# K's, V's and the late weights' loads issued by GpSimd, one packet per DMA engine, in a decode kernel with attention and a gated MLP

## The chip, the cores and the metric

The kernel runs on one core of one Trainium2 chip. The time is the device time in microseconds of one execution; the median of three runs of the kernel before is 2520.21 us (2520.2 to 2520.8). A profile of one execution shows what each engine did: TensorE (PE, with its weight loads PEld), VectorE (DVE), ScalarE (ACT), GpSimd (POOL), SyncE (SP), and the 16 DMA engines that move data between HBM and the on-chip memory.

## The reference

One token passes two branches, mixed by a gate. The attention branch reads a long cache: 32 heads, 65,536 cached tokens, 128 numbers each, in bfloat16, so K and V together are 1.07 GB that have to be read once.

```python
q = (x @ wq).reshape(B, Sq, H, Dh).transpose(0, 2, 1, 3)       # one token, H = 32, Dh = 128
scores = einsum("bhqd,bhkd->bhqk", q, k_cache) * Dh ** -0.5    # Sk = 65536
a = (softmax(scores) @ v_cache -> reshape) @ wo                # D = 512
b = (silu(x @ w_gate) * (x @ w_up)) @ w_down                   # F = 1792
g = sigmoid((x * gate_w).sum(-1))
out = g * a + (1 - g) * b
```

## The kernel before

The tokens of a head are split into two halves, z = 0 and z = 1, of 32,768 tokens. A half of K or of V is one load of 8 MiB: 128 partitions, each with a contiguous row of 256 tokens (64 KiB). All loads go into one large buffer `mem`, in blocks of 512 numbers per partition; `place` (L193 to L196) gives the block of each load. K's first half goes to block 32 (KA), K's second to 0 (KZ), V's first half to 120 (VA) and V's second to 96 (VZ). VA and VZ overlap by 40 blocks, KZ and KA by 32, so a load has to wait until the part that it overwrites has been used.

Work on a head runs as a software pipeline over the engines. VectorE transposes K in eight steps per half (L397 and L404; L329 for the first head), each into one of two buffers `kt`, and counts them in the semaphore `ktdone`. TensorE multiplies each transposed step with the query (L454, `scores`) and counts in `qkdone`. When both halves of a head have their scores, VectorE takes the maximum per partition (L343), GpSimd the maximum over the partitions (L273, `partition_all_reduce`), ScalarE the exponentials (L300) with their sums, and GpSimd the sum over the partitions (L275). VectorE rearranges the exponentials into `pb` with 16 small copies per half (L338, `shuffle`). TensorE then multiplies them with V of that head (L501), one head behind the scores, in two parts per half, and counts the parts in `pvdone`; `turn` (L481) and two ScalarE steps bring the head's result into a column.

The order of the loads is written out on SyncE (L209 to L245). The four weight loads `wq`, `wg`, `wu`, `wd` are issued ahead of everything (L203), then K's first half for head 0 in two loads of 4 MiB (L217), and then for each head, each behind a wait on `ktdone` or `pvdone`: K's first half, V's first half of the head before, K's second half, V's second half of the head before (all L213). The loads of the end are: 31 of the 32 rows of `wo` (L235), the last head's V in eight pieces from 4 MiB down to 128 KB (L242, table `tail`), and two loads of 128 KB from `wo` (L244, L245). All of these share one queue, SP's. ScalarE issues the token `x`, `gate_w` and the output.

GpSimd at the start builds small constants (L249 to L269, with `affine_select`), then does only the two reductions per head, in the order of heads (L272 to L275). VectorE and TensorE run their heads in a loop on their engine; what they wait for is given by counts of the semaphores.

Of the kernel before, what the change touches and what calls it, by code (L numbers as in the profile page):

```python
# [5 lines left out]
P = 128  # L6
KB = 512
PR = 32
NG = PR // 4

ALU = mybir.AluOpType
ACT = mybir.ActivationFunctionType
# [8 lines left out]
def bass_gated_mix__mha_block_cached__swiglu_ffn__decode_kernel(  # L21
# [11 lines left out]
    out: bass.AP,  # L33
):
    _, H, S, Dh = A_k_cache.shape
    D = A_wq.shape[0]
    F = B_w_gate.shape[1]
# [3 lines left out]
    HR = R // 2  # L41
    NP = HR // PR
# [5 lines left out]
    KA, KZ, VA, VZ, V0 = 32, 0, 120, 96, 96  # L48
# [10 lines left out]
    tail = [(32, 0, 128), (0, 128, 128), (V0 + 24, 256, 128), (V0 + 64, 384, 64),  # L59
            (V0 + 80, 448, 32), (V0 + 56, 480, 16), (V0 + 60, 496, 12), (V0 + 63, 508, 4)]  # L60
    WOJ, WO31 = V0, V0 + 1

    with ExitStack() as ctx:
# [6 lines left out]
        def sem(name):  # L70
            return ctx.enter_context(nc.semaphore(name))
# [35 lines left out]
        def at(kb, n):  # L107
            return mem[:, kb * KB:kb * KB + n]
# [9 lines left out]
        d = {n: sem("d_" + n) for n in names}  # L118
        dt_ = [sem(f"d_t{i}") for i in range(len(tail))]
# [16 lines left out]
        s_q = sem("s_q")  # L136
# [7 lines left out]
        s_b = sem("s_b")  # L144
        s_dch = sem("s_dch")
        ktdone = sem("ktdone")
        qkdone = sem("qkdone")
        pvdone = sem("pvdone")
# [26 lines left out]
        w_dram = {  # L175
            "wq": A_wq.rearrange("(p c) n -> p (c n)", c=Dc),
            "wg": B_w_gate.rearrange("(p c) f -> p (c f)", c=Dc),
            "wu": B_w_up.rearrange("(p c) f -> p (c f)", c=Dc),
            "wd": B_w_down.rearrange("(p c) n -> p (c n)", c=FC),
            "wo": A_wo.rearrange("(p j) n -> p (j n)", p=P),  # L180
        }
        wj_dram = w_dram["wo"][:, 31 * D:32 * D]
        w31_dram = A_wo.rearrange("(h d) n -> h d n", d=Dh)[H - 1]
        WQ, WG, WU, WD, WO = V0, 0, 14, V0 + 64, 64
# [5 lines left out]
        w2_ap = at(WOJ, 2 * D).rearrange("p (e c n) -> p e c n", e=2, c=4)  # L190
        ktb = [kt[:, b, :].bitcast(BF16).rearrange("p (j r m e) -> p j r m e", j=2, r=NG, e=2) for b in range(2)]

        def place(kind, h, z):  # L193
            if kind == "k":
                return (KA, V0)[z] if h == 0 else (KA, KZ)[z]
            return (VA, VZ)[z]  # L196

        def kv_dram(cache, h):
            return cache[0, h].rearrange("(b p r) d -> b p (r d)", b=2, p=P)

        for n, kb in (("wq", WQ), ("wg", WG), ("wu", WU), ("wd", WD)):
            src = w_dram[n]
# [3 lines left out]
        ctx.callback(lambda: nc.scalar.wait_ge(s_out, 16))  # L206
        block = ctx.enter_context(nc.Block())

        @block.sync  # L209
        def _(sp):  # L210
            def load(kind, h, z):
                cache = A_k_cache if kind == "k" else A_v_cache
                sp.dma_start(at(place(kind, h, z), HR * Dh), kv_dram(cache, h)[z]).then_inc(d[kind + "az"[z]], 16)  # L213

            half = HR // 2 * Dh
            for n in range(2):
                sp.dma_start(at(KA + 32 * n, half), kv_dram(A_k_cache, 0)[0][:, n * half:n * half + half]).then_inc(  # L217
                    (d["ka0"], d["ka"])[n], 16)
            sp.wait_ge(s_q, 1)
            load("k", 0, 1)  # L220
            for h in range(1, H):
                sp.wait_ge(ktdone, 2 * NP * h - 3 if h > 1 else NP)
                load("k", h, 0)
                if h == 1:
                    sp.wait_ge(ktdone, 2 * NP - 3)
                    sp.wait_ge(s_b, 1)
                else:
                    sp.wait_ge(pvdone, 4 * h - 1)
                load("v", h - 1, 0)
                sp.wait_ge(ktdone, 2 * NP * h + NP // 2)  # L230
                load("k", h, 1)
                sp.wait_ge(pvdone, 4 * h + 1)
                load("v", h - 1, 1)
            sp.wait_ge(ktdone, 2 * NP * H - NP)
            sp.dma_start(at(WO, 31 * D), w_dram["wo"][:, 0:31 * D]).then_inc(d["wo"], 16)  # L235
            src = A_v_cache[0, H - 1].rearrange("(b p r) d -> b p (r d)", b=2, p=P)
            need = {0: (ktdone, 2 * NP * H - 3), 1: (ktdone, 2 * NP * H), 2: (pvdone, 4 * H - 1)}
            for n, (kb, r0, nr) in enumerate(tail):
                if n in need:
                    sp.wait_ge(*need[n])  # L240
                b, o = divmod(r0, HR)
                sp.dma_start(at(kb, nr * Dh), src[b][:, o * Dh:(o + nr) * Dh]).then_inc(dt_[n], 16)  # L242
            sp.wait_ge(pvdone, 4 * H)
            sp.dma_start(at(WOJ, D), wj_dram).then_inc(d["wj"], 16)  # L244
            sp.dma_start(at(WO31, D), w31_dram).then_inc(d["w31"], 16)  # L245

        @block.gpsimd
        def _(pool):
            nc.gpsimd.memset(onesf[0:1, :], 1.0)  # L249
            nc.gpsimd.memset(sel, 0.0).then_inc(s_sel0, 1)  # L250
            pool.wait_ge(s_sel0, 1)
            for je in range(4):
                off = 64 * (je // 2) + je % 2
                v = sel[:, je, :].rearrange("p (g d) -> p g d", g=4)
                last = nc.gpsimd.affine_select(out=v, in_=v, compare_op=ALU.not_equal, fill=1.0, base=-off,
                                               pattern=[[0, 4], [-2, 32]], channel_multiplier=1)
            last.then_inc(s_sel, 1)
            nc.gpsimd.memset(unit[:], 0.0).then_inc(s_unit0, 1)
            pool.wait_ge(s_unit0, 1)
            nc.gpsimd.affine_select(out=unit[:], in_=unit[:], compare_op=ALU.not_equal, fill=1.0, base=0,  # L260
                                    pattern=[[-1, 4]], channel_multiplier=1).then_inc(s_unit, 1)
            nc.gpsimd.memset(bmat[:], 0.0).then_inc(s_b0, 1)
            for q in range(4):
                pool.wait_ge(s_b0, q + 1)
                nc.gpsimd.affine_select(out=bmat[:], in_=bmat[:], compare_op=ALU.not_equal, fill=1.0, base=-32 * q,
                                        pattern=[[-1, 32]], channel_multiplier=1).then_inc(s_b0, 1)
            nc.gpsimd.memset(hot[0:1, :, :], 0.0).then_inc(s_hot0, 1)
            pool.wait_ge(s_hot0, 1)
            nc.gpsimd.affine_select(out=hot[0:1, :, :], in_=hot[0:1, :, :], compare_op=ALU.not_equal, fill=1.0,  # L269
                                    base=0, pattern=[[1, 4], [-1, 4]], channel_multiplier=0).then_inc(s_hot, 1)  # L270
            for h in range(H):
                pool.wait_ge(s_mx, h + 1)  # L272
                nc.gpsimd.partition_all_reduce(amx, mxs, P, RMAX).then_inc(s_ar, 1)  # L273
                pool.wait_ge(expdone, h + 1)
                nc.gpsimd.partition_all_reduce(Lt, rsum, P, RADD).then_inc(s_L, 1)  # L275

        @block.scalar
        def _(act):
# [148 lines left out]
        def _(pe):  # L427
# [22 lines left out]
            def scores(z, c, u):  # L450
                col = 256 * z + PR * u
                for r in range(NG):
                    for je in range(4):
# [129 lines left out]
```

## Time and profile before

| | |
|---|---|
| median of three runs | 2520.21 us |
| span of the profiled execution, first to last instruction | 2518.7 us |
| the profiled execution's own time | not given apart from its span; the median lies 1.5 us above the span |
| moved by the DMA engines | 1088.00 MB, mean 432 GB/s |
| share of the 16 engines' span, SP's queue | 99.9% |
| PE, DVE, ACT, POOL busy | 63%, 55%, 3%, 1% |
| PE weight loads busy | 35% |
| mean granted TensorE clock | 0.711 |
| loads of 8 MiB, K and V | 63 and 62 |

A line of the timeline gives the start in us from the span's beginning, the duration, the engine and line, the operation, what it writes and reads, and in brackets how long the engine stood idle before it and what ended that wait. SPq is SP's issuing of a DMA. A line of the DMA issues ends with the time in us from the issue to the landing of the data. In the chain of waits a line is a start, a length and what the chain went through in that time. A group of instructions gives busy time, mean duration in ns, and the idle time ahead of it with its releaser.

### The profile page before, as it was taken

The page shows a single profiled execution, that of the slowest core. Times are in us where ns is not written, and L with a number is a line of the kernel's source. Part 1 is how long each engine was busy: PE and PEld are TensorE (multiplying, and loading weights), DVE is VectorE, ACT ScalarE, POOL GpSimd, SP SyncE. Part 2 cuts the span into 40 slices and gives each one's busy share as a digit, 9 for nine tenths or more (in the row PEclk, how much of TensorE's full clock was granted, in tenths as well). Part 3 has the DMA queues.
Part 4 walks back from the last instruction along what each step waited for, and adds up shares of the span by engine and source line. Part 5 has one row for each costly group of instructions (what it writes and reads, how often), then busy time and mean ns, then how long its engine had stood idle before and what let it go on. Part 6 is the DMA issues. An engine that isn't in the chain of part 4 may idle for free.

```text
span 2518.7 us, 46364 instructions
## 1 busy us (share of the span) xinstructions
PE 1584.6 (63%) x21432; PEld 890.1 (35%) x21432; DVE 1397.8 (55%) x1630; ACT 65.6 (3%) x195; POOL 27.0 (1%) x83
## 2 busy tenths in 40 slices
PE   3556756657666566565675665766656656567567
PEld 3333333333333333333333333333333333333334
DVE  3764565554654645646446555466464564644653
ACT  0000000000000000000000000000000000000000
POOL 0000000000000000000000000000000000000000
PEclk8567767677676776676776767767767767677676
DMA  9999999999999999999999999999999999999999
GB/s 421 432 433 434 434 434 433 433 433 433 433 433 433 433 433 434 433 436 433 433 434 432 433 434 433 433 433 434 433 433 433 437 434 433 433 433 434 433 433 390
DMA packets 20477, 1088.00 MB, mean 432 GB/s; under 512 B 2283, under 2 KB 2669, under 8 KB 2925
## 3 DMA queue, kind: packets, MB, share of 16 engines
q1 hardware_dynamic: 20448, 1087.78, 99.9%
q8 instruction: 11, 0.18, 0.0%
q14 instruction: 6, 0.04, 0.0%
q10 hardware_dynamic: 12, 0.00, 0.0%
HBM read 1087.77 MB, written 0.00 MB: 432 GB/s over the span
## 4 chain that ended last, share of the span: by engine, by line
DMA 73%; DVE 14%; issue 11%; PE 1%; DVEq 0%; SPq 0%; ACT 0%
DMA mem<-in_A_k_cache_dram 71%; DVE kt L404 7%; DVE kt L397 6%; DMA mem<-in_A_wo_dram 1%; PE psO L501 1%; DMA mem<-in_A_v_cache_dram 1%; DVE kt L329 0%; DVE pb L338 0%; DVEq L402 0%; SPq L203 0%; DVEq L395 0%; PE psZ L552 0%; PE psS L454 0%; SPq L217 0%; ACT fin L307 0%
## 5 line engine op out<-in xcount | busy, mean ns | idle before, releaser
L454 PE MATMUL psS<-qcur,kt 128*128 128x4 bf16 x16384 | 516.9, 166 | 887.0 <-DVE kt L397 552.5
L501 PE MATMUL psO<-mem,pb 128*4 128x512 bf16 x3968 | 999.8, 417 | 17.1 <-DMA mem<-in_A_v_cache_dram 17.1
L397 DVE STREAM_TRANSPOSE kt<-mem 128x2048 uint32<-128x2048 uint32 x248 | 551.2, 2280 | 578.5 <-DMA mem<-in_A_k_cache_dram 577.4
L454 PEld LDWEIGHTS psS<-qcur,kt 128*128 128x128 bf16 x16384 | 474.3, 104 | 955.7 <-DVE kt L397 585.7
L404 DVE STREAM_TRANSPOSE kt<-mem 128x2048 uint32<-128x2048 uint32 x248 | 547.6, 2275 | 407.5 <-DMA mem<-in_A_k_cache_dram 407.5
L501 PEld LDWEIGHTS psO<-mem,pb 128*4 128x4 bf16 x3968 | 354.3, 91 | 619.1 <-issue 186.2
L338 DVE COPY pb<-pa 32x64 bf16<-32x64 bf16 x1024 | 233.7, 228 | 25.9 <-PE psO L501 11.1
L329 DVE STREAM_TRANSPOSE kt<-mem 128x2048 uint32<-128x2048 uint32 x16 | 35.4, 2279 | 16.9 <-DMA mem<-in_A_k_cache_dram 16.9
L343 DVE TENSOR_REDUCE sm<-psS 128x1 f32<-128x512 f32 x32 | 22.1, 692 | 35.5 <-PE psS L454 35.5
L294 ACT ACTIVATE oTn<-psT,gcol 128x1 bf16<-128x1 f32 x31 | 8.2, 263 | 1111.6 <-PE psT L481 1111.6
L273 POOL PARTITION_ALL_REDUCE sm<-sm x32 | 11.3, 352 | 2391.2 <-DVE sm L343 2391.2
L481 PEld LDWEIGHTS psT<-unit,orow 4*128 4x128 f32 x256 | 30.8, 186 | 14.9 <-issue 13.5
L481 PE MATMUL psT<-unit,orow 4*128 4x1 f32 x256 | 33.5, 248 | 0.8 <-ACT orow L292 0.8
L292 ACT ACTIVATE orow<-psO,sm 4x512 f32<-4x512 f32 x31 | 21.0, 678 | 446.8 <-issue 446.8
L298 ACT ACTIVATE sm<-sm 128x1 f32<-128x1 f32 x32 | 6.5, 203 | 832.1 <-POOL sm L273 832.1
L300 ACT ACTIVATE pa<-psS,sm 128x512 bf16<-128x512 f32 x32 | 22.0, 687 | 1.0
L515 PE MATMUL psW<-pb,mem 128*128 128x1 bf16 x512 | 14.3, 165 | 7.1 <-DMA mem<-in_A_v_cache_dram 6.0
L515 PEld LDWEIGHTS psW<-pb,mem 128*128 128x128 bf16 x512 | 13.9, 102 | 8.1 <-issue 6.4
L275 POOL PARTITION_ALL_REDUCE sm<-sm x32 | 12.3, 385 | 36.4 <-ACT pa L300 36.4
L438 PE MATMUL psM<-xTb,mem 128*128 128x1 bf16 x128 | 3.6, 165 | 11.5 <-DMA mem<-in_A_wq_dram 11.5
L424 DVE TENSOR_SCALAR w<-psW,sm 128x4 bf16<-128x4 f32 x1 | 0.2, 226 | 17.5 <-PE psW L515 17.5
L466 PE MATMUL psM<-xTb,mem 128*128 128x1 bf16 x112 | 6.9, 198 | 4.6 <-DMA mem<-in_B_w_up_dram 4.6
(63 smaller groups left out, 64.1 us busy)
## 6 DMA issues: line engine op xcount, KB each, us to landing
mem<-in_A_v_cache_dram SPq DMA_DIRECT2D x3, 4096.0 KB, 27.8
mem<-in_A_k_cache_dram SPq DMA_DIRECT2D x2, 4096.0 KB, 38.9
mem<-in_A_wq_dram SPq DMA_DIRECT2D x1, 4096.0 KB, 13.0
mem<-in_A_wo_dram SPq DMA_DIRECT2D x1, 3968.0 KB, 33.8
mem<-in_A_v_cache_dram SPq DMA_DIRECT2D x1, 2048.0 KB, 32.3
mem<-in_B_w_gate_dram SPq DMA_DIRECT2D x1, 1792.0 KB, 16.9
mem<-in_B_w_up_dram SPq DMA_DIRECT2D x1, 1792.0 KB, 21.4
mem<-in_B_w_down_dram SPq DMA_DIRECT2D x1, 1792.0 KB, 25.2
```

Source lines behind the costliest of these rows:

```text
L275: nc.gpsimd.partition_all_reduce(Lt, rsum, P, RADD).then_inc(s_L, 1)
L292: nc.scalar.mul(orow[0:4, :], psO[0:4, :], Li[0:4, :]).then_inc(s_or, 1)
L300: nc.scalar.activation(pa[:], psS[:], ACT.Exp, bias=nbias, scale=SCALE, accum_out=rsum).then_inc(expdone, 1)
L329: nc.vector.transpose(kt[:, i % 2, :].rearrange("p (j r t) -> p r j t", j=2, t=32), src.rearrange("p (r j t) -> p r j t", j=2, t=32)).then ...
L338: last = nc.vector.tensor_copy(dst, sr)
L343: nc.vector.reduce_max(mxs, psS[:], AX_X).then_inc(s_mx, 1)
L397: nc.vector.transpose(kt[:, c % 2, :].rearrange("p (j r t) -> p r j t", j=2, t=32), src.rearrange("p (r j t) -> p r j t", j=2, t=32)).then ...
L404: nc.vector.transpose(kt[:, c % 2, :].rearrange("p (j r t) -> p r j t", j=2, t=32), src.rearrange("p (r j t) -> p r j t", j=2, t=32)).then ...
L454: last = nc.tensor.matmul(psS[:, col + 4 * r:col + 4 * r + 4], ktb[c % 2][:, je // 2, r, :, je % 2], qcur[:, je, :], start=(je == 0), stop ...
L481: last = nc.tensor.matmul(psT[:, 0:1], orow[0:4, i * Dh:(i + 1) * Dh], unit[0:4, i:i + 1], start=(i == 0), stop=(i == 3))
L501: last = nc.tensor.matmul(psO[0:4, :], pb[:, 256 * z + r:256 * z + r + 4], vt[:, r * Dh:(r + 4) * Dh], start=(z == 0 and part == 0 and m = ...
L515: last = nc.tensor.matmul(psW[:, 0:1], vt[:, r * Dh:(r + 1) * Dh], pb[:, col:col + 1], start=(col == 0), stop=(col == R - 1))
```

## The change

The program on SyncE after the four weight loads goes away. GpSimd issues the same loads in the same order behind the same waits, with software-made descriptors, and each of them with `single_packet=True`, which marks all that one DMA engine moves for the load as one packet. `load` becomes a function that takes the engine. The two reductions of a head become a function `peaks`, and GpSimd's program has them between the loads: for head 0 behind the first V load, for the others between K's and V's first half, and for the last head behind the wait of the third V piece. One wait is new: GpSimd waits until `wu` has landed before it issues the first K load. The weight loads, `x`, `gate_w` and the output stay where they were.

```diff
-        @block.sync
-        def _(sp):
-            def load(kind, h, z):
-                cache = A_k_cache if kind == "k" else A_v_cache
-                sp.dma_start(at(place(kind, h, z), HR * Dh), kv_dram(cache, h)[z]).then_inc(d[kind + "az"[z]], 16)
...
+        def load(eng, kind, h, z):
+            cache = A_k_cache if kind == "k" else A_v_cache
+            eng.dma_start(at(place(kind, h, z), HR * Dh), kv_dram(cache, h)[z],
+                          single_packet=ONE).then_inc(d[kind + "az"[z]], 16)
...
-            for h in range(H):
+            def peaks(h):
                 pool.wait_ge(s_mx, h + 1)
                 nc.gpsimd.partition_all_reduce(amx, mxs, P, RMAX).then_inc(s_ar, 1)
                 pool.wait_ge(expdone, h + 1)
                 nc.gpsimd.partition_all_reduce(Lt, rsum, P, RADD).then_inc(s_L, 1)
+            half = HR // 2 * Dh
+            pool.wait_ge(d["wu"], 16)
+            for n in range(2):
+                pool.dma_start(at(KA + 32 * n, half), kv_dram(A_k_cache, 0)[0][:, n * half:n * half + half],
+                               single_packet=ONE).then_inc((d["ka0"], d["ka"])[n], 16)
+            pool.wait_ge(s_q, 1)
+            load(pool, "k", 0, 1)
+            for h in range(1, H):
+                pool.wait_ge(ktdone, 2 * NP * h - 3 if h > 1 else NP)
+                load(pool, "k", h, 0)
+                if h == 1:
+                    pool.wait_ge(ktdone, 2 * NP - 3)
+                    pool.wait_ge(s_b, 1)
+                    load(pool, "v", 0, 0)
+                    peaks(0)
+                else:
+                    peaks(h - 1)
+                    pool.wait_ge(pvdone, 4 * h - 1)
+                    load(pool, "v", h - 1, 0)
+                pool.wait_ge(ktdone, 2 * NP * h + NP // 2)
+                load(pool, "k", h, 1)
+                pool.wait_ge(pvdone, 4 * h + 1)
+                load(pool, "v", h - 1, 1)
...
+            for n, (kb, r0, nr) in enumerate(tail):
+                if n in need:
+                    pool.wait_ge(*need[n])
+                if n == 2:
+                    peaks(H - 1)
...
```

More of the change, by code (lines that the diff above doesn't have):

```diff
@@ L9 @@
 NG = PR // 4
+ONE = True
 ALU = mybir.AluOpType
@@ L207, in bass_gated_mix__mha_block_cached__swiglu_ffn__decode_kernel @@
         block = ctx.enter_context(nc.Block())
-        @block.sync
-        def _(sp):
-            def load(kind, h, z):
-                cache = A_k_cache if kind == "k" else A_v_cache
[L213 to L245, printed above, removed]
+        def load(eng, kind, h, z):
+            cache = A_k_cache if kind == "k" else A_v_cache
+            eng.dma_start(at(place(kind, h, z), HR * Dh), kv_dram(cache, h)[z],
+                          single_packet=ONE).then_inc(d[kind + "az"[z]], 16)
         @block.gpsimd
@@ L275, in _ @@
                 nc.gpsimd.partition_all_reduce(Lt, rsum, P, RADD).then_inc(s_L, 1)
+            half = HR // 2 * Dh
[21 more added lines that the diff above has]
+                load(pool, "v", h - 1, 1)
+            pool.wait_ge(ktdone, 2 * NP * H - NP)
+            pool.dma_start(at(WO, 31 * D), w_dram["wo"][:, 0:31 * D], single_packet=ONE).then_inc(d["wo"], 16)
+            src = A_v_cache[0, H - 1].rearrange("(b p r) d -> b p (r d)", b=2, p=P)
+            need = {0: (ktdone, 2 * NP * H - 3), 1: (ktdone, 2 * NP * H), 2: (pvdone, 4 * H - 1)}
+            for n, (kb, r0, nr) in enumerate(tail):
[3 more added lines that the diff above has]
+                    peaks(H - 1)
+                b, o = divmod(r0, HR)
+                pool.dma_start(at(kb, nr * Dh), src[b][:, o * Dh:(o + nr) * Dh], single_packet=ONE).then_inc(dt_[n], 16)
+            pool.wait_ge(pvdone, 4 * H)
+            pool.dma_start(at(WOJ, D), wj_dram, single_packet=ONE).then_inc(d["wj"], 16)
+            pool.dma_start(at(WO31, D), w31_dram, single_packet=ONE).then_inc(d["w31"], 16)
         @block.scalar
```

## The prediction

> **What bounds the kernel now.** I read the page's queue part and its slices first, then the chain of waits, then one head in the timeline, then the start and the end of the span.
>
> The page: the DMA slices, the queues, and two groups of instructions.
>
> ```profile
> DMA packets 20477, 1088.00 MB, mean 432 GB/s; under 512 B 2283, under 2 KB 2669, under 8 KB 2925
> q1 hardware_dynamic: 20448, 1087.78, 99.9%
> q8 instruction: 11, 0.18, 0.0%
> DMA 73%; DVE 14%; issue 11%; PE 1%; DVEq 0%; SPq 0%; ACT 0%
> L397 DVE STREAM_TRANSPOSE kt<-mem 128x2048 uint32<-128x2048 uint32 x248 | 551.2, 2280 | 578.5 <-DMA mem<-in_A_k_cache_dram 577.4
> L273 POOL PARTITION_ALL_REDUCE sm<-sm x32 | 11.3, 352 | 2391.2 <-DVE sm L343 2391.2
> ```
>
> One queue, SP's, carries 99.9% of the 16 engines' span. DVE idles 578.5 us at L397 for K alone; the chain is 73% DMA. Only what changes the DMA stream changes the end.
>
> One head, from the timeline: SP's issues, DVE, and POOL.
>
> ```profile
> 1590.59 0.33 SPq L213 DMA_DIRECT2D mem<-in_A_v_cache_dram  x1
> 1595.17 17.66 DVE L404 STREAM_TRANSPOSE kt<-mem 128x2048 uint32<-128x2048 uint32 x8 [13.13 <-DMA mem<-in_A_k_cache_dram]
> 1606.28 0.33 SPq L213 DMA_DIRECT2D mem<-in_A_k_cache_dram  x1
> 1614.73 0.35 POOL L273 PARTITION_ALL_REDUCE sm<-sm  x1 [75.54 <-DVE sm L343]
> 1616.22 0.38 POOL L275 PARTITION_ALL_REDUCE sm<-sm  x1 [1.14 <-ACT pa L300]
> 1625.36 0.33 SPq L213 DMA_DIRECT2D mem<-in_A_v_cache_dram  x1
> ```
>
> The chain of waits in order of time has the same step every head, here two heads 29 apart, and the time from issue to landing of the two K loads of a head.
>
> ```profile
> 94.60 29.67 DMA mem<-in_A_k_cache_dram
> 1606.28 27.50 DMA mem<-in_A_k_cache_dram
> 2339.89 29.67 DMA mem<-in_A_k_cache_dram
> ```
>
> (2339.89 - 94.60) / 29 = 77.42 us per head, four loads of 8 MiB: 19.356 us each, with the queue never empty. A load that lands 29.67 us after its issue has waited about 10.3 us in the queue: that is its cover. The other K load has 27.5 - 19.36 = 8.1, V's first half (27.8 us in the per-line answers) 8.4, V's second half, issued at 1590.59, lands after 23.8 us and has only 4.4. That last one is the thin place.
>
> The start, and the end, from the DMA issues and the timeline.
>
> ```profile
> mem<-in_B_w_up_dram SPq DMA_DIRECT2D x1, 1792.0 KB, 21.4
> mem<-in_B_w_down_dram SPq DMA_DIRECT2D x1, 1792.0 KB, 25.2
> 37.03 8.89 DVE L329 STREAM_TRANSPOSE kt<-mem 128x2048 uint32<-128x2048 uint32 x4 [5.65 <-DMA mem<-in_A_k_cache_dram]
> 46.74 4.50 DVE L329 STREAM_TRANSPOSE kt<-mem 128x2048 uint32<-128x2048 uint32 x2 [0.82 <-DMA mem<-in_A_k_cache_dram]
> 2510.67 0.51 PE L515 MATMUL psW<-pb,mem 128*128 128x1 bf16 x13 [1.25 <-DMA mem<-in_A_v_cache_dram]
> 2512.33 2.78 PE L515 MATMUL psW<-pb,mem 128*128 128x1 bf16 x99 [1.16 <-issue]
> 2515.41 0.58 PE L515 MATMUL psW<-pb,mem 128*128 128x1 bf16 x16 [0.30 <-DMA mem<-in_A_v_cache_dram]
> ```
>
> **What a load costs beside its bytes.** The two 4 MiB halves of K's first block land 46.74 - 37.03 = 9.71 us apart; 8 MiB takes 19.356. So 2 x 9.71 - 19.356 = 0.06 us of a load does not grow with its bytes, and 4 MiB of bytes take 9.65. In the tail, pieces 3 and 6 land at about 2510.67 and 2515.41: 4.74 us for three loads of 1024, 512 and 384 KB, whose bytes take 4.52; 0.22 / 3 = 0.07 each. Against this, the last three loads of 128 KB land with about 0.3 us each, which is their bytes alone. I take 0.07 us. What is it made of? q1's 20448 packets are 142 loads x 144: 128 rows and 16 small ones, so nine packets per engine and load. If the 0.07 us belongs to packet boundaries, each is 8 ns.
>
> **The change, part by part.** The sum is made against the profiled span of 2518.7 us; the median of the runs, 2520.2, lies 1.5 us above, and I carry that over unchanged.
>
> 1. *One packet per engine.* 138 of the 142 loads move (2 + 63 + 62 of K and V, 1 + 8 + 2 at the end); nine packets become one, or two if the completion stays apart. Upper end: 138 x 0.07 x 8/9 = 8.6 us saved. Lower end: 0, if the constant belongs to a load's completion, or a loss of the same size, 9.7 us, if software descriptors double it. The large loads, 128 of 138, are the rows nearest, and they show the constant whole; the tiny ones do not. I take three quarters: -6.5 us. [...]
>
> 2. *Issuing on GpSimd.* SP's 0.33 us per issue goes away; POOL issues 138 more instructions, each waiting in order. K's first half (1606.28) is followed by the maximum at 1614.73: 8.4 us of room. The sum at L275 ends at 1616.60 and V's first half is due at 1625.36: 8.8 us. So neither the reductions nor the loads wait for each other until one issue costs POOL over 8 us; price 0. For the first head, POOL's pause before its second kind of instruction (12.6 us idle before L255, put down to "issue", is the only such pause shown) follows V's load at 77.21 and could end at 90.2, with the maximum due at 85.70. exp would then end near 92 instead of 87.1; DVE needs it at 94.50 and K's next issue is due at 94.60, so it is still covered.
>
> 3. *Later start of a transfer.* No software-issued load is in this trace. From issue to landing, beyond the bytes, hardware issue takes between 1.4 us (x, 1 KB, issued 0.73, used 2.16) and 13.0 - 9.65 = 3.3 (wq). Cover is 4.4 to 10.3 us, so software may add 1.1 us by the one and 3.0 by the other before an engine runs dry. I take one microsecond more than hardware issue, under the lower bound, because V's second half is issued while DVE and POOL are idle: price 0. With the cover gone, every further microsecond costs one per head, 31 us.
>
> 4. *The wait for wu at the start.* wu lands at 1.63 + 21.4 = 23.0, wd at 2.12 + 25.2 = 27.3. K's first half is now issued at 23.0 instead of 2.70, so 4.3 us of wd cover it, the same margin as in 3: 0, at most some 1.5 us once. Behind that wait on POOL stand only the loads; psM's users and DVE get their data in the same order.
>
> 5. *The order at the end.* POOL waits for PV (127) before the last maximum: 2478.0 instead of 2466.64, so exp and the 16 copies (3.96 us) end near 2483.4; the second 16 start at 2483.15 anyway. PE's first piece waits for its load until 2485.5, and PE idles 3.8 us before piece 2 at 2505.86. Price 0. Piece 2's issue moves from 2477.97 by the 1.9 us of maximum, exp and sum; it landed 27.8 us after issue, 18 more than its bytes.
>
> 6. *Other queues behind long packets.* q8's 11 instruction fetches share the engines. Beside 32 KB packets the 1 KB of gate_w, issued at 1.29, was used only at 8.21: some 5.5 us lost to others' packets. A packet is now up to 8 rows, 9.7 or 19.4 us. Price between 0 and 11 us (rival 3); I take 1, the size of the fetch stall that PE already shows (1.16 us before 2512.33).
>
> Sum: -6.5 + 0 + 0 + 0 + 0 + 1 = -5.5: span 2513.2, time 2514.7 us.
>
> **The rivals.**
>
> 1. *The constant belongs to the load, not to the packets.* The tiny loads, with nine packets each and no constant, speak for it; then part 1 is worth nothing and the time is 2520 + 0 to 2, 2516 to 2524 with the smaller shares of part 1.
>
> 2. *Software issue is too late for V's second half* (slower). For: it has the thinnest cover, 4.4 us, 31 times, and nothing here shows what descriptor writing for 128 rows costs. Against: PE's work between K's landing and this issue is fixed (1556.48 to 1590.59, 34 us), so a gap does not grow. It decides from 1.1 to 3.0 us of extra latency. With 2 us too much: 62 us more, less 6.5: 2576; with half a microsecond: 2529.
>
> 3. *Instruction fetches wait for whole packets.* PE fetched at 49.0, 58, 66, 81 and 88 us, while K's first blocks landed. If a fetch near 58 waits for the rest of a 19.4 us load, PE's scores of the second half stop up to 15 us; V's first load (77.21, cover 8.4) is then late and the engines dry for 7 to 9 us, once, and 0 to 2 at the end: -6.5 + 9 + 1: 2524, range 2516 to 2535. For: gate_w's 5.5 us. Against: the blocks are fetched about one ahead, and from 90 us to 2490 there is no q8 fetch at all. [...]
>
> **How the numbers follow.** A measurement of this kernel tells about 0.2% (5.0 us) from no change: 2515.2 to 2525.2. The forecast holds 0.44, 2509.5 to 2516 as its own range (0.40 below 2515.2, 0.04 within). Rival 1: 0.16, all within. Rival 3: 0.20, 0.08 within and 0.12 above. Rival 2: 0.20, above. Faster 0.40, same 0.28, slower 0.32. The range runs from 2509.5 (all of the 8.6 us and a little) to 2545, which leaves out 0.04 below and some 0.12 of rival 2 above.
>
> **What would show it.** Part 1: a software queue with far fewer packets, and a head period near 77.2 instead of 77.42; at 77.42, rival 1. Part 3 and rival 2: V's second half landing without or with a drop in the DMA share; a period of 78 or more, and a longer wait of PE for V, prove me wrong. Part 4: wd used as before near 31.5, K's first half near 37. Part 6 and rival 3: PE idle for "issue" between 50 and 100 us, and a slice below 430 GB/s there.

## The result

The changed kernel takes 2530.86 us (median of 4 runs, 2523.34 to 2533.46) against 2520.2 us before (2519.75 to 2520.8). The ratio is 1.0038, with a 95% interval of 1.0026 to 1.005: slower, by 0.3 to 0.5%, where 2514.7 us was forecast. New is also the spread: over all runs on record the kernel before stays within 2519.6 and 2522.6 us, the changed one lies anywhere between 2522.8 and 2535.8. The profile belongs to the shortest of the four runs, 2523.34 us, so this trace explains 3 us of the loss and another one must explain the rest.

The page of the changed kernel: packets, queues, the chain, and the groups that answer to those shown of before.

```profile
DMA packets 20124, 1088.00 MB, mean 431 GB/s; under 512 B 2282, under 2 KB 2284, under 8 KB 2572
q0 software_dynamic: 19520, 1078.08, 98.9%
q1 hardware_dynamic: 576, 9.70, 0.9%
q8 instruction: 11, 0.18, 0.0%
DMA 72%; DVE 14%; issue 12%; PE 1%; DVEq 0%; POOL 0%; ACT 0%; SPq 0%
L403 DVE STREAM_TRANSPOSE kt<-mem 128x2048 uint32<-128x2048 uint32 x248 | 551.3, 2280 | 579.9 <-DMA mem<-in_A_k_cache_dram 578.1
L212 POOL DMA_DIRECT2D mem<-in_A_v_cache_dram x62 | 34.0, 548 | 1045.1 <-PE psO L507 996.8
L212 POOL DMA_DIRECT2D mem<-in_A_k_cache_dram x63 | 33.5, 531 | 1010.2 <-DVE kt L403 507.4
```

The loads have moved to a software queue, q0, but they have not become fewer packets: 19520 are 138 loads of 144, less 352. The 352 are missing at four small loads of the end: rows of 1 KB now come four to a packet of 4 KB (three loads, 288 fewer; the packets under 2 KB went from 386 to 2), and rows of 3 KB two to a packet (64 fewer). The kernel without the mark, below, has the same packets, so that joining comes with the software queue and not with the mark. A load of 64 KB rows is still 128 packets and 16 small ones of 4 bytes. An issue costs GpSimd 0.53 us, well under the 8 us of room.

Three steps of its chain of waits: the same K load 25 heads apart, and the last load.

```profile
173.77 29.39 DMA mem<-in_A_k_cache_dram
2109.49 29.39 DMA mem<-in_A_k_cache_dram
2486.00 33.12 DMA mem<-in_A_wo_dram
```

(2109.49 - 173.77) / 25 = 77.43 us per head, against 77.42 before. In a head without a disturbance the stream is exactly as fast as it was.

The start, and one late issue, from the timeline of the changed kernel.

```profile
23.10 1.41 POOL L248 DMA_DIRECT2D mem<-in_A_k_cache_dram  x2 [6.27 <-DMA mem<-in_B_w_up_dram]
38.37 8.89 DVE L335 STREAM_TRANSPOSE kt<-mem 128x2048 uint32<-128x2048 uint32 x4 [7.21 <-DMA mem<-in_A_k_cache_dram]
2211.36 1.05 PE L487 MATMUL psT<-unit,orow 4*128 4x1 f32 x8
2214.40 0.53 POOL L212 DMA_DIRECT2D mem<-in_A_v_cache_dram  x1 [26.82 <-issue]
2216.41 17.66 DVE L410 STREAM_TRANSPOSE kt<-mem 128x2048 uint32<-128x2048 uint32 x8 [13.13 <-DMA mem<-in_A_k_cache_dram]
```

K's first piece is used at 38.37 instead of 37.03 us: 1.3 us lost. Near 2214 us GpSimd issues V's second half 3 us after the part of PV that releases it (PE is at `turn`, which follows it, at 2211.36), and the load lands about 1 us late. Together with 0.55 us near 2014 us, where the kernel before loses 0.3 us too, that is the 3 us of this run.

### The profile page after: what moved, and what is told of

The parts are those of the page before. It is cut to its first block, busy times and chain, and to the rows that moved or that the text cites. A ratio compares the mean times of both kernels' runs of the same rounds, so it can differ in the third digit from the quotient of the medians.

```text
span 2521.8 us, 46365 instructions
## 1 busy us (share of the span) xinstructions
PE 1588.8 (63%) x21432; PEld 890.7 (35%) x21432; DVE 1398.7 (55%) x1630; ACT 65.6 (3%) x195; POOL 101.4 (4%) x221
## 2 busy tenths in 40 slices
DMA packets 20124, 1088.00 MB, mean 431 GB/s; under 512 B 2282, under 2 KB 2284, under 8 KB 2572
## 3 DMA queue, kind: packets, MB, share of 16 engines
q0 software_dynamic: 19520, 1078.08, 98.9%
## 4 chain that ended last, share of the span: by engine, by line
DMA 72%; DVE 14%; issue 12%; PE 1%; DVEq 0%; POOL 0%; ACT 0%; SPq 0%
DMA mem<-in_A_k_cache_dram 69%; DVE kt L410 7%; DVE kt L403 6%; DMA mem<-in_A_wo_dram 1%; PE psO L507 1%; DMA mem<-in_A_v_cache_dram 1%; DMA mem<-in_B_w_up_dram 1%; DVE kt L335 1%; PE psS L460 0%; DVE pb L344 0%; DVEq L408 0%; POOL mem L248 0%; DVEq L401 0%; PE psZ L558 0%; SPq L204 0%
## 5 line engine op out<-in xcount | busy, mean ns | idle before, releaser
L212 POOL DMA_DIRECT2D mem<-in_A_v_cache_dram x62 | 34.0, 548 | 1045.1 <-PE psO L507 996.8
L212 POOL DMA_DIRECT2D mem<-in_A_k_cache_dram x63 | 33.5, 531 | 1010.2 <-DVE kt L403 507.4
L444 PE MATMUL psM<-xTb,mem 128*128 128x1 bf16 x128 | 3.6, 165 | 11.4 <-DMA mem<-in_A_wq_dram 11.4
```

The costliest lines, as they stand in the source:

```text
L212: eng.dma_start(at(place(kind, h, z), HR * Dh), kv_dram(cache, h)[z], single_packet=ONE).then_inc(d[kind + "az"[z]], 16)
```

## The experiments

In what follows the *cover* of a load is the time from its issue to the landing of the load ahead of it, and its *gap* is the time between the two landings less 19.356 us, the time of 8 MiB in the undisturbed stream. Both are worked out per load, in the text from the issue times in the timeline and the times to landing in the per-line answers, which are rounded to 0.1 us, and in the tables from the unrounded times of the same traces.

### The changed kernel again, and the same without the mark

```diff
-ONE = True
+ONE = False
```

For the unchanged repetition:

> The changed kernel once more, for the spread of its times and a second trace. Profiled so far: 2521.8 us of span, head period 77.43 us as before, +1.3 to 1.8 us at the start, +1.0 us at one late issue of GpSimd at 2214 us; its other runs lay at 2528 to 2533 us. Theory A (late issues): a trace of 2528 us or more shows several issues of V's second half on GpSimd that come microseconds after their wait was over, each followed by a gap of the DMA engines of about 1 to 10 us, and heads without one still take 77.43 us. Theory B (slower stream): the head period is longer in every head, 77.6 to 77.75 us, with no late issue.

For the kernel without the mark:

> GpSimd issues, but without the mark of one packet per engine. Theory A (issuing on GpSimd costs it): the same as the changed kernel, 2522 to 2534 us, start 1.3 us late, period 77.43 us. Theory B (the mark costs it): back to 2520 to 2523 us in all runs. If the mark did help the stream, this kernel is slower than the changed one by up to 9 us.

Measured: repetition 2531.67 us (2522.80 to 2535.75, 6 runs), without the mark 2531.59 us (2523.41 to 2534.20, 6 runs). The mark is worth nothing, either way: the packets are 20124 in both. The repetition's trace was again of its shortest run (2522.8 us). The trace without the mark is of a run of 2530.36 us, and shows what such a run is made of. Its timeline in one head:

```profile
199.92 0.53 POOL L212 DMA_DIRECT2D mem<-in_A_v_cache_dram  x1 [24.89 <-PE psO L507]
204.00 17.66 DVE L410 STREAM_TRANSPOSE kt<-mem 128x2048 uint32<-128x2048 uint32 x8 [13.09 <-DMA mem<-in_A_k_cache_dram]
224.32 6.04 PE L507 MATMUL psO<-mem,pb 128*4 128x512 bf16 x19 [1.59 <-DMA mem<-in_A_v_cache_dram]
```

V's second half is issued at 199.92, K's second half lands at 203.91: 4.0 us of cover. It should land 19.36 us after K, at 203.91 + 19.36 = 223.27; it lands at 224.32, a gap of 1.05 us, and PE waits for it. In this trace the gaps of all loads behind the first one of V sum to 8.1 us, and 6.5 of them fall on ten loads of V's second half. With the 2.2 us by which that first V load itself lands later than before, they make up the 10.2 us by which the span of this execution, 2528.9 us, is longer than the 2518.7 of before. All ten had a cover of 4.64 us or less (one, near 2221 us, is the late issue); loads with nearly the same cover have none (4.04 us: 0.00). So for the mark theory A held: without it the kernel is the same. Of the repetition's two theories neither held whole: the issues were not late, as theory A had it, and the stream was not slower in every head, as theory B had it. Most of the gaps sit at the one load with the least cover, now and then.

### Only the new wait, and only the mark, on SP

```diff
             half = HR // 2 * Dh
+            sp.wait_ge(d["wu"], 16)
```

> The kernel before, with only the new wait: SP waits for wu before its first K load. If the late start of the changed kernel is the wait's, K's first half lands near 38.3 us and the time is +1.3 us (2521.5 us). If it is the first software issue's own latency (15.3 us from issue to landing against 9.7 of bytes), K's first half lands near 37.0 us and the time is 2520.2 us.

```diff
-                sp.dma_start(at(place(kind, h, z), HR * Dh), kv_dram(cache, h)[z]).then_inc(...)
+                sp.dma_start(at(place(kind, h, z), HR * Dh), kv_dram(cache, h)[z], single_packet=True).then_inc(...)
```

> The kernel before, SP issuing as before, with the mark of one packet on K's and V's 8 MiB loads. If packet boundaries were the 0.07 us constant of a load, 125 loads save up to 7.8 us: 2512 us. If the mark is worth nothing, the period stays 77.42 us and the time 2520.2 us. If the mark itself is what spreads the changed kernel's runs, this one spreads over 2523 to 2533 us as well.

Measured: with the wait 2520.22 us (2519.81 to 2520.65, 11 runs; ratio 1.0001, 0.9992 to 1.0009), K's first piece used at 37.14. So the wait costs 0.1 us, and the other 1.2 us of the start belong to the first software issue: 15.3 us from issue to use, of which 9.65 are bytes. (In the other traces of GpSimd's kernel with this wait the first piece lands 0.8 to 2.1 us later than in this one of SP, so the 1.3 us are one value of several.) With the mark 2520.0 us (2519.73 to 2520.66, 11 runs; ratio 1.0000, 0.9991 to 1.0009), 20476 packets as before. The mark did nothing on hardware issue either.

### What the constant of a load is

Three variants of the kernel before. One deals the tokens of a half to the partitions in two stretches, so that a load has 256 rows of 32 KB instead of 128 of 64 KB (the attention sums over all tokens, and K and V are dealt alike). One does the same bytes as two loads of 4 MiB. One cuts only V's second half, which is also the control for the next section.

```diff
-            return cache[0, h].rearrange("(b p r) d -> b p (r d)", b=2, p=P)
+            return cache[0, h].rearrange("(b c p r) d -> b p c (r d)", b=2, c=2, p=P)
```

> The kernel before, with the tokens of a half dealt to the partitions in two stretches: a load has the same bytes, but 256 rows of 32 KB in place of 128 of 64 KB, so 16 packets per engine in place of 8, and as many loads as before. If the 0.07 us of a load are 8 ns per packet, 125 loads x 8 packets x 8 ns = 8 us more: 2528 us. If they belong to the load, or to nothing of the kind, 2520.2 us.

```diff
-                sp.dma_start(at(place(kind, h, z), HR * Dh), kv_dram(cache, h)[z]).then_inc(d[kind + "az"[z]], 16)
+                for c in range(2):
+                    sp.dma_start(at(place(kind, h, z) + 32 * c, half), kv_dram(cache, h)[z][:, c * half:c * half + half]).then_inc(
+                        d[kind + "az"[z]], 16)
```

> The kernel before, every K and V half (beside the first of head 0 and the last V) as two loads of 4 MiB with rows of 32 KB. If the cost sits in each row (9.3 ns, completions alike), this is the kernel with 32 KB rows plus one completion per engine and load: 2529.4 + 125 x 9.3 ns = 2530.6 us. If it sits in the load, 0.07 us for each of 125 more loads on top of 2529.4: 2538 us.

Measured: rows of 32 KB 2529.43 us (2529.15 to 2529.48, 5 runs; ratio 1.0037, 1.0024 to 1.005); two loads 2529.79 us (2529.53 to 2530.17, 5 runs; ratio 1.0038, 1.0024 to 1.0052). The page of the kernel with 32 KB rows, and its chain:

```profile
DMA packets 36476, 1088.00 MB, mean 430 GB/s; under 512 B 2282, under 2 KB 2668, under 8 KB 2924
172.50 29.82 DMA mem<-in_A_k_cache_dram
2037.63 29.85 DMA mem<-in_A_k_cache_dram
```

16000 more packets, 1000 per engine, cost 9.4 us: 9.4 ns per row. Per head it is (2067.48 - 202.32) / 24 = 77.72 us, 0.30 more for 32 rows per engine. Twice as many completions (the packets of 4 bytes, one per engine and load) add only 0.4 us more, 2529.79 against 2529.43. So the constant of a load belongs to its rows, as rival 1 denied and part 1 assumed; what failed is that the mark does not join them.

### More cover for V's second half

In the changed kernel, V's second half is cut in two: the 3 MiB that overwrite nothing of V's first half are issued right behind K's second half, and 5 MiB behind the old wait.

```diff
                 load(pool, "k", h, 1)
+                pool.wait_ge(pvdone, 4 * h)
+                cut = V_KEEP * Dh
+                src = kv_dram(A_v_cache, h - 1)[1]
+                pool.dma_start(at(VZ, cut), src[:, 0:cut], single_packet=ONE).then_inc(d["vz"], 16)
                 pool.wait_ge(pvdone, 4 * h + 1)
-                load(pool, "v", h - 1, 1)
+                pool.dma_start(at(VA, HR * Dh - cut), src[:, cut:HR * Dh], single_packet=ONE).then_inc(d["vz"], 16)
```

> The changed kernel, with V's second half loaded in two pieces: 3 MiB as soon as K's second half is issued, 5 MiB behind the old wait. That gives the late piece 7 us more cover; one more load per head. Theory A (the thin cover of V's second half, 4 to 5.6 us, is at times too short for a software issue): the spread of 2523 to 2536 us ends, all runs 2521.5 to 2524 us. Theory B (the software stream itself is slower in most executions, wherever the loads are issued): the spread stays, median about 2531 us. If 0.07 us belongs to every load, 31 more loads cost 2.2 us in either.

The same cut with SP issuing:

> The kernel before with V's second half in two pieces, as in the split kernel on GpSimd. Nine more packets per engine and head at 9.3 ns: 31 x 9 x 9.3 ns = 2.6 us more, 2522.8 us, and nothing gained from the better cover, because hardware issue left no gap. The split kernel on GpSimd (2524.8 us) then costs 2.0 us more than this one: 1.3 us at the start and the rest in the late issue near 2214 us. If GpSimd's loads were slower in the stream too, the difference would be larger, 4.5 us or more.

Measured: on GpSimd 2524.78 us (2524.29 to 2526.41, 11 runs; ratio 1.002, 1.0011 to 1.0029), on SP 2522.32 us (2522.24 to 2522.51, 10 runs; ratio 1.0009, 0.9999 to 1.0018). The spread of 10 us is gone, with the mark still on and all loads still on GpSimd. Beyond the rows that the cut adds (2.3 us on SP; the expectation's 2.6 us counted the completion like a row), issuing on GpSimd costs 2.5 us when the cover is ample, 1.3 of them at the start; behind the first V load, none of K's and V's loads of 31 heads leaves a gap over 0.15 us in either trace. The late issue, which the expectation has near 2214 us, is at 1786.67 us in this kernel and leaves no gap. The issues of one head:

```profile
275.79 0.53 POOL L271 DMA_DIRECT2D mem<-in_A_v_cache_dram  x1 [23.13 <-PE psO L511]
281.14 17.67 DVE L414 STREAM_TRANSPOSE kt<-mem 128x2048 uint32<-128x2048 uint32 x8 [13.06 <-DMA mem<-in_A_k_cache_dram]
300.51 16.63 PE L511 MATMUL psO<-mem,pb 128*4 128x512 bf16 x64 [0.63 <-DMA mem<-in_A_v_cache_dram]
```

Behind K's landing at 281.02 the whole of V's second half is there 19.4 us later, although its late piece was issued, as ever, 5.2 us ahead of K's landing: 3 MiB of it already stood in the queue.

### No cover at all: the latency of an issue

Both kernels with V's second half issued one part of PV later.

```diff
-                sp.wait_ge(pvdone, 4 * h + 1)
+                sp.wait_ge(pvdone, 4 * h + 2)
```

> The kernel before, with V's second half issued one part of PV later (pvdone 4h+2), some 6.4 us, so that it comes 1 to 2 us after K's second half has landed, in all 31 heads. Every head then shows the whole latency of a hardware issue as a gap. Taking it as 1.4 to 3.3 us from the first loads: a gap of about 3 to 5 us per head, 93 to 155 us in all, 2613 to 2675 us.

> The changed kernel with the same later issue. The difference of its head period to that of the kernel with the late issue on SP is the extra latency of a software issue. Theory A: 1 to 2.5 us more per head, varying from head to head, and from run to run by 10 us and more. Theory B: no extra latency, the same period within 0.3 us.

Measured: on SP 2644.49 us (2642.99 to 2645.99, 2 runs; ratio 1.0494, 1.0475 to 1.0513), on GpSimd 2664.88 us (2664.54 to 2666.44, 4 runs; ratio 1.0577, 1.0561 to 1.0593). One head of each, SP's first (PE's part ends at 282.45 + 5.34 = 287.79), then GpSimd's (285.20 + 5.34 = 290.54):

```profile
282.45 5.34 PE L501 MATMUL psO<-mem,pb 128*4 128x512 bf16 x24
287.83 0.33 SPq L213 DMA_DIRECT2D mem<-in_A_v_cache_dram  x1
309.73 2.72 PE L501 MATMUL psO<-mem,pb 128*4 128x512 bf16 x6 [3.41 <-DMA mem<-in_A_v_cache_dram]
```

```profile
285.20 5.34 PE L507 MATMUL psO<-mem,pb 128*4 128x512 bf16 x24
290.84 0.53 POOL L212 DMA_DIRECT2D mem<-in_A_v_cache_dram  x1 [30.60 <-PE psO L507]
313.02 3.57 PE L507 MATMUL psO<-mem,pb 128*4 128x512 bf16 x8 [5.07 <-DMA mem<-in_A_v_cache_dram]
```

SP issues 0.04 us after the part has ended, GpSimd 0.30 us after. From there to landing, beyond the bytes, hardware takes 2.44 us (median of 29 heads, 2.24 to 2.74) and software 2.74 (30 heads, 2.54 to 3.14). Software is later by 0.26 + 0.30 = 0.56 us; the times give (2664.88 - 2644.49 - 1.3) / 31 = 0.62. That lies between the two theories, and it is steady. On an idle queue, then, 4 us of cover would be plenty. The gaps come from something else than this latency alone.

### A little less cover

Both kernels with the issue put behind `turn`, about 1.1 us later.

```diff
                 sp.wait_ge(pvdone, 4 * h + 1)
+                sp.wait_ge(s_pt, h)
```

> The changed kernel with V's second half issued about 1.1 us later, behind turn (4 short multiplications after the first part of PV): cover 2.9 to 4.6 us in place of 4.0 to 5.7. From the latencies on an idle queue (2.44 us hardware, 2.74 us software) a cover of 2.9 us would still be enough. Theory C (a software issue against a running stream needs up to 5.3 us, at random): gaps in most heads, 0.3 to 2 us each, 15 to 40 us above the lowest 2523 us, in every run. Theory D (the gaps are not tied to the cover): the same 2523 to 2536 us as before.

> The kernel before with the same 1.1 us of delay. Theory C: hardware issue needs 2.44 us, so a cover of 2.9 us and more leaves no gap: 2520 to 2521 us. If hardware too needs more against a running stream than on an idle queue, gaps appear here as well: 2525 us or more.

Measured: on GpSimd 2544.88 us (2539.86 to 2546.49, 5 runs; ratio 1.009, 1.0076 to 1.0103), on SP 2534.12 us (2533.04 to 2536.08, 4 runs; ratio 1.0055, 1.0039 to 1.007). Hardware issue has the gaps too. A head of SP's kernel:

```profile
588.71 0.33 SPq L213 DMA_DIRECT2D mem<-in_A_v_cache_dram  x1
592.66 17.66 DVE L405 STREAM_TRANSPOSE kt<-mem 128x2048 uint32<-128x2048 uint32 x8 [13.21 <-DMA mem<-in_A_k_cache_dram]
```

Cover 3.8 us, and the load lands 25.0 us after its issue, near 613.7: a gap of 1.8 us. Over the 31 heads of each trace:

| trace | cover of V's second half, us | heads with a gap over 0.2 us | sum of these gaps, us |
|---|---|---|---|
| before | 4.31 to 5.94 | 0 of 31 | 0 |
| before with the mark, on SP | 4.30 to 5.95 | 1 of 31 (cover 4.39) | 0.3 |
| changed, 2523.34 us | 1.89 (the late issue), 3.27 to 5.94 | 1 of 31 | 1.0 |
| without the mark, 2530.36 us | 2.51 (the late issue), 3.97 to 5.76 | 10 of 31 | 6.5 |
| behind `turn`, SP | 2.92 to 5.00 | 11 of 31 | 12.7 |
| behind `turn`, GpSimd | 0.91 (the late issue), 2.88 to 4.44 | 15 of 31 | 21.3 |

Above 4.7 us V's second half has no such gap in any head of these traces; below, some heads have one and some have none, whoever issues. The kernel before, with covers from 4.31 us, already has heads below that edge.

The traces also hold each packet by itself, and these tell why the same cover can have a gap in one head and none in another. The 16 engines do not end a load together: the first of them is through 0.7 to 3.9 us before the load lands, so for that engine the cover, which counts to the landing, is too long by as much. The time that matters is the one from the issue to the moment when the first engine runs out of rows. Over the 310 loads of V's second half in ten traces (before, with the wait and with the mark on SP, behind `turn` twice, and five of GpSimd's kernel, two of them from the sections below):

| first engine out of rows after the issue | loads | engines without a row, over 0.3 us in sum | gap over 0.2 us |
|---|---|---|---|
| less than 1.5 us | 52 | 52 | 28 |
| 1.5 to 2.5 us | 81 | 25 | 15 |
| more than 2.5 us | 177 | 1 | 3 |

This fits the kernels with no cover, where the first row starts 0.96 us after a hardware issue and 1.24 us after a software one, and the last engine's first row 1.4 to 2.1 and 1.7 to 2.4 us after. In the kernel before, engines that started late but were ahead of the others made no gap: at its least cover, 4.31 us, two engines were free at 2367.36 and 2367.51 us and got their next row at 2367.61 and 2367.64, the last engine came free at 2369.11, and the load landed on time.

### Without the wait for wu

```diff
-            pool.wait_ge(d["wu"], 16)
```

> The changed kernel without the wait for wu: GpSimd issues K's first half as soon as its constants are built, near 17 us, while three weight loads are still in SP's queue. If a marked load keeps the engines until its 256 KB per engine are through, wu and wd come 10 to 20 us later, the MLP with them, and the time is 2 to 10 us above the changed kernel's lowest 2523 us. If the engines take rows of both queues in turn, wu and wd come 4 to 6 us later, which PE and DVE hide, and the 1.3 us at the start are saved: runs from 2521.5 us up.

Measured: 2522.82 us (2521.97 to 2532.73, 7 runs; ratio 1.0022, 1.001 to 1.0035). K's first piece is used at 36.98 again, so the 1.3 us are won back, and the spread stays. The DMA issues and the timeline of this kernel at the start:

```profile
mem<-in_A_k_cache_dram POOLq DMA_DIRECT2D x2, 4096.0 KB, 24.3
mem<-in_B_w_up_dram SPq DMA_DIRECT2D x1, 1792.0 KB, 23.0
mem<-in_B_w_down_dram SPq DMA_DIRECT2D x1, 1792.0 KB, 36.6
24.81 6.85 PE L471 MATMUL psM<-xTb,mem 128*128 128x1 bf16 x112 [6.34 <-DMA mem<-in_B_w_up_dram]
36.98 4.50 DVE L334 STREAM_TRANSPOSE kt<-mem 128x2048 uint32<-128x2048 uint32 x2 [3.94 <-DMA mem<-in_A_k_cache_dram]
38.74 5.79 PE L479 MATMUL psY<-mem,guT 128*1 128x512 bf16 x14 [7.08 <-DMA mem<-in_B_w_down_dram]
```

wu landed in the midst of K's marked load, at 24.6 instead of 23.0, and wd 14.1 us later instead of 4.3. Eight rows of wd (0.53 us each) and eight of K (1.2 us each) in turn make 13.9 us. So the marked load did not hold the engines; the rows of the two queues alternated. That wd came 11 us later, not 4 to 6, cost nothing: PE and DVE made it up.

### Once more for the trace

> The changed kernel once more for its trace. If it falls above 2528 us: gaps at loads of V's second half that were issued 4.0 to 4.7 us before K's second half had landed, summing to the excess over 2523 us, and none at the loads with 7 us of cover or more. Below 2524 us: no such gaps.

Measured: 2526.21 us, between the two cases, and a trace between them: gaps over 0.2 us at V's second half with covers of 4.00 (0.28 us), 4.08 (1.38) and 4.46 (0.32), the late issue at 2217.00 (0.75), and at two loads with ample cover (0.20 at 57.88, 0.67 at 2016.59), which the expectation did not have. Together 3.6 us, against 1.5 in the trace of 2523.34 us: 2.1 of the 2.9 us between the two runs; K's first piece lands 0.6 us later too. So this longer run of the marked kernel is made of the same gaps as the run without the mark. None of its runs above 2530 us is traced.

## Why the prediction was wrong

**Part 1 failed, and with it the sign.** The constant of a load and its split into rows were read rightly (8 ns per packet from the trace of before, 9.4 ns measured). That the mark would make one packet of a load's nine was taken from its name; the packet counts and two kernels, 2531.59 us without the mark on GpSimd and 2520.0 with it on SP, show that it does not. Its -6.5 us is 0. That takes the forecast to 2521, no change; that the kernel is slower comes from parts 3 and 4. Rival 1 named the right outcome, that part 1 is worth nothing, with the wrong reason.

**Part 2 held.** 0.53 us per issue, reductions and loads do not wait for each other; GpSimd's pause before the first maximum ended at 89.86 us, near the 90.2 bound, and was hidden.

**Part 3 and rival 2: the place was right, the edge was wrong.** V's second half is where the loss comes from: more cover there ends it. But the part priced it at 0 by setting a latency (1.4 to 3.3 us) against the cover (4.4 us) and leaving 1.1 us for software. Software took only 0.56 us more; that DVE and POOL are idle at this issue, the part's reason for one microsecond, was tried by no run. What was not seen is that in the running stream of these traces covers of up to 4.6 us left gaps, although the latency on an idle queue is 2.44 us: the first engine runs out up to 3.9 us before the landing to which the cover counts. The kernel before already stood at 4.31. A shift of half a microsecond was enough: 6.5 us of gaps at V's second half in the trace of 2530.36 us, where the sum had 0. The forecast "one microsecond per head for each microsecond too much" had a sharp edge; the real one is blurred: at a cover of 2.9 to 4.6 us, 0 to 2.8 us per head. That rival 2's time for half a microsecond, 2529, lies near the 2530.86 measured is luck: it takes off the 6.5 us of part 1, and it counts the half microsecond in every head.

**Part 4 was mis-sized:** 0 taken, 1.5 us as the bound, 1.3 measured in the trace of 2523.34 us and 2.2 in that of 2530.36, from the first software issue and not from the wait.

**Part 5 held:** the last maximum moved to 2480.62, and piece 2 still waited for its load.

**Part 6 and rival 3 fell.** The q8 fetches start at 50.5, 58.4, 65.8, 81.3 and 91.1 us, each within about 3 us of the one before the change, and without the wait for wu the rows of two queues came in turn (13.9 us by their sum, 14.1 measured), although one of the two loads was marked. Before the change two of the fetches, at 58.99 and 66.29 us, start while PE waits for VectorE's transposes until 68.47, so they come ahead of PE's need, as rival 3 says against itself. The mark did not change what the profile counts as a packet: 20124 with it and without it.

## What to carry to other kernels

When a stream is at its limit, look at the smallest cover of any load, less the time by which the first engine ends ahead of the others (0.7 to 3.9 us here), and set the latency of an issue against that: the kernel before stood right at the edge, at 4.31 us, and showed nothing, and 0.56 us of latency more left 6.5 us of gaps at that load in the run of 2530.36 us. Cutting the load so that its unconflicted part is issued early bought cover cheaply here, 2.3 us of extra rows for 7 us of cover. And a flag that should merge transfers is tested by counting packets, here 20124 with it and without it, before its gain is put in a sum. No kernel tried here was faster than the one before.

## What the runs showed that was not expected

- A load that is issued 2.9 to 4.6 us ahead of the landing before it leaves a gap of up to 1.8 us (hardware) or 2.8 us (software) in some heads and none in others, while a load issued onto an idle queue lands 2.2 to 2.7 us (hardware) beyond its bytes. The engines' different ends, above, explain most of this. Why the first engine is 0.7 us ahead of the landing at one time and 3.9 at another, and why some executions have ten gaps and others one, stays open. So do the gaps of 0.2 to 0.7 us at loads with 7 us of cover and more: up to seven in a trace, 2.5 us in sum (behind `turn` on GpSimd).
- In all eight traces of a kernel with these loads on GpSimd the 115th load that GpSimd issues comes 2.9 to 3.2 us after what it waits for, the others some 0.3 to 0.9; the profile calls the reason "issue". With four loads per head it is V's second half, between 2211 and 2342 us; in the kernel with V's second half in two pieces, five loads per head, it comes at 1786.67 us. So it goes with the number of loads issued, not with the time or the head; 114 loads are 1026 packets per engine. It costs 0.5 to 1.0 us in the traces of the changed kernel. What GpSimd waits for there stays open.
- A row costs its engine 9.4 ns beside its bytes, and a completion some 3 ns (0.4 us for 125 more per engine).
